# Two groups of eight head slots run as one matmul run, with the second group on the other column tiles and another PSUM bank

## The chip, the cores and the metric

The kernel runs on one core of one Trainium2 chip. The metric is the time of one execution on the device in microseconds (us), lower is better. Three runs of the kernel before gave 1065.8, 1064.63 and 1068.15 us; the median is 1065.8.

## The reference

Three stages follow one another: a delta-rule attention over 4 x 8 heads, 768 tokens and a head size of 48, and two feed-forward layers over all 3072 tokens (width 384, inner width 2048).

```python
# attention: B, H, S, D = 4, 8, 768, 48
k_n = k / (np.linalg.norm(k, axis=-1, keepdims=True) + 1e-06)
for t in range(S):
    y[:, :, t] = np.einsum('bhd,bhde->bhe', q[:, :, t], state)
    v_old = np.einsum('bhde,bhd->bhe', state, kt)
    state = state + bt[:, :, :, None] * np.einsum('bhd,bhe->bhde', kt, vt - v_old)
# first layer:  h = x @ w_in;  g = h / (1 + exp(-1.702 h));  x = g @ w_out
# second layer: h = max(x @ w_in, 0);  out = (h * h) @ w_out
```

## The kernel before

**Chunks and slots.** The 768 tokens are cut into 12 chunks of 64. The 32 heads sit as 16 slots of two heads: of one slot, one head has partitions 0 to 63 and the other 64 to 127. The 16 slots are two groups of eight (`g` 1 and 0), or four quarters of four. All the matmuls of the attention are fp32; each of them shows as two MATMUL instructions in the trace, so a run of 16 matmuls is "x32" there.

**One chunk of the attention** takes these steps on TensorE (PE); the letters are used in the rest of the text.

- **a** (`run_a`): keys and queries against keys, 64 x 64 tiles with 128 columns, one run of 8 matmuls for each of the four quarters; ScalarE (ACT) then copies 6 pieces out of PSUM for each. `load_kq` fetches a quarter (256 KB).
- the triangular solve: `solve_in` and `solve_norm` on VectorE (DVE), `solve_prep` (its last writes are those of `U`), `solve_loop` on GpSimd (POOL; 31 pairs of operations for chunks 4 to 11), then `finish`, whose last operation on DVE writes `Td`.
- **x** (`run_x`): the state's old prediction, 48 x 64 tiles; DVE subtracts it from `v_sb`.
- **W0**, **W1** (`run_w`, k = 0 and 1): the solved block `Td` against `v_sb`, 32 x 32 tiles; ACT copies four pieces of 32 partitions into `ws`.
- **G** (`run_g`), between the two: 32 x 32 tiles; four subtractions of 32 partitions on DVE.
- **y** (`run_y`): the output of the chunk, 128 rows x 48 columns, both column halves in turn.
- **s** (`run_s`): the new state, 64 x 48 tiles; four additions on DVE into `ws`.

In x, W0, G, W1 and s the loop `for g, ps, A, sl in groups()` makes one run of 16 matmuls for each group, into one of three PSUM banks (`a0` to `a2`, for chunks 2 and up) that `bank()` hands out in turn. Within such a run two tiles alternate: the head in the lower rows and the head in the upper rows, which write to different column halves.

```python
for g, ps, A, sl in groups():              # run_w
    for p in range(8):
        for h in range(2):
            r = 64 * h + 32 * k
            todo.append((ps[r:r + 32, p, :], Td[r:r + 32, 8 * g + p, :], v_sb[r:r + 32, 8 * g + p, :], True, True))
    mms((0.64, 0.82), todo, [("Td", n % 2), ("v", g, k)], [A], 0.25)
```

**The layers.** `step` issues the 9 matmuls of `h` (128 x 512; 128 x 256 at the start) for one slice of the inner width, and `layer2` the 9 of `z`. The results go through ACT (`g`, `ghi`) and DVE (`g`, `glo`) between the two. These large matmuls of the first layer are mixed with the attention of later chunks; `run_items` places the steps of a chunk at fixed steps of the layer (`TUNE["scan"]`, `TUNE["solve"]`, `gscan`, `gsolve`).

**The order.** Nothing is issued directly: every operation is put into `Program` with its cost, and `flush` writes the order of each engine out as a list scheduler that goes by these costs (for matmuls the first number given to `mms`, the second is the cost at the lower clock). Each engine then works through its list in order, so an instruction that waits holds up all that stand behind it on its engine.

Of the kernel before, what the change touches and what calls it, by code (L numbers as in the profile page):

```python
# [190 lines left out]
def kernel(  # L191
    ctx: ExitStack,
    tc: tile.TileContext,
    kq: bass.AP,
# [194 lines left out]
    def run_a(n, g, nxt=None):
        (t, keys), i = kq_of.pop((n, g)), n % 2  # L390
        G = G_sb[i]
        ps, A = bank(8 if n < 2 else 3)
        mms(0.87, [(ps[64 - r:128 - r, 128 * p:128 * p + 128], t[r:r + 64, 0, p, :], t[r:r + 64, :, p, :], True, True)
                  for p in range(4) for r in (64, 0)], keys + (["first"] if n == 1 else []), [A])
        if nxt:
            load_kq(*nxt)
        v4 = ps.rearrange("p (a c t) -> p a c t", a=4, c=2)
        sl = slice(4 * g, 4 * g + 4)
        for r in range(0, 128, 32):
            if r % 64 == 0:  # L400
                copy(256, [A], [("G", i, g, r)], G[r:r + 32, sl, :], v4[r:r + 32, :, 0, :])
            else:
                copy(128, [A], [("G", i, g, r)], G[r:r + 32, sl, 0:32], v4[r:r + 32, :, 0, 32:64])
        for h in range(2):
            r = 64 * h
            copy(256, [A], [("P", h, i, g)], pq[h][i][r:r + 64, sl, :], v4[r:r + 64, :, 1, :], early=-TUNE["p_late"] if n < 2 else 0)
        if g == 3 and n > 1:
            for h in range(2):
                mask_P(n, h)
# [198 lines left out]
    def groups():  # L608
        for g in (1, 0):
            ps, A = bank()  # L610
            yield g, ps[:, 0:8 * D].rearrange("p (a d) -> p a d", a=8), A, slice(8 * g, 8 * g + 8)

    def run_x(n):
        for g, ps, A, sl in groups():
            todo = []
            for p in range(8):
                a = 8 * g + p
                todo.append((ps[0:64, p, :], kT_sb[64:112, a // 4, a % 4, :], ws[0][64:112, a, :], True, True))
                todo.append((ps[64:128, p, :], kT_sb[0:48, a // 4, a % 4, :], ws[1][0:48, a, :], True, True))
            mms((1.24, 1.3), todo, KT + [("S", g)], [A], 0.2)  # L620
            tt(8 * D, [A], [("v", g, 0), ("v", g, 1)], v_sb[:, sl, :], v_sb[:, sl, :], ps, ALU.subtract)

    def run_w(n, k):
        Td = Td_sb[n % 2]
        for g, ps, A, sl in groups():
            todo = []
            for p in range(8):
                for h in range(2):
                    r = 64 * h + 32 * k
                    todo.append((ps[r:r + 32, p, :], Td[r:r + 32, 8 * g + p, :], v_sb[r:r + 32, 8 * g + p, :], True, True))  # L630
            mms((0.64, 0.82), todo, [("Td", n % 2), ("v", g, k)], [A], 0.25)
            for h in range(2):
                r = 64 * h + 32 * k
                copy(8 * D, [A], [("W", g, k, h)], ws[h][r:r + 32, sl, :], ps[r:r + 32], ("act", "dve") if n == 0 else "act")

    def run_g(n):
        G = G_sb[n % 2]
        for g, ps, A, sl in groups():
            todo = []
            for p in range(8):  # L640
                for h in range(2):
                    r = 64 * h
                    todo.append((ps[r + 32:r + 64, p, :], G[r:r + 32, 8 * g + p, 32:64], ws[h][r:r + 32, 8 * g + p, :], True, True))
            mms((0.43, 0.43), todo, G_keys(n) + [("W", g, 0, 0), ("W", g, 0, 1)], [A], 0.25)
            for h in range(2):
                r = 64 * h + 32
                tt(8 * D, [A], [("v", g, 1)], v_sb[r:r + 32, sl, :], v_sb[r:r + 32, sl, :], ps[r:r + 32], ALU.subtract)
# [33 lines left out]
    def run_s(n):  # L681
        for g, ps, A, sl in groups():
            todo = []
            for p in range(8):
# [4 lines left out]
            for h in range(2):
                q = 64 - 64 * h  # L690
                if n == 0:
                    act(8 * D, [A], [("S", g)], out=ws[h][q:q + 48, sl, :], in_=ps[q:q + 48])
# [90 lines left out]
    with tc.manual_schedule():  # L783
# [11 lines left out]
        for g in range(4):  # L795
# [13 lines left out]
        for g in range(4):  # L809
# [200 lines left out]
```

## Time and profile before

| | |
|---|---|
| median of three runs | 1065.8 us (1064.63 to 1068.15) |
| profiled execution, first to last instruction (span; the profile lists no other time of it) | 1063.8 us |
| PE busy | 1019.1 us, 96% |
| DVE / ACT / POOL busy | 587.3 (55%) / 529.5 (50%) / 326.6 us (31%) |
| mean granted TensorE clock, share of full | 0.977 |
| large matmuls `h` and `z` of 128 x 512, one | 0.38 to 0.42 us busy, a new one each 0.23 us |
| last attention matmul (chunk 11's y) | begins at 578.5 us |

Busy time of one matmul is longer than its share of the engine, since matmuls overlap: it is the distance between starts that counts. A line "x32" of the timeline is a run of 32 instructions from the first start to the modelled end of the last. In brackets stands the idle time before a line and what ended it.

### The profile page before, as it was taken

Reading aid. Unit: us, or ns where it says so; the run is one execution under the profiler, and the core shown is the slowest. Engines: PE = TensorE matmul, PEld = TensorE weight load, DVE = VectorE, ACT = ScalarE, POOL = GpSimd, SP = SyncE. Lnnn points to the kernel's source line nnn. Section 1 sums busy time; section 2 is a strip of 40 time slices with the busy share of each in tenths; the row PEclk is TensorE's granted clock in tenths of the full one; section 3 lists DMA queues with packets and bytes.
Section 4 is the critical chain, followed back from the end, with each engine's and each line's share of the span. In section 5 each row is a group of like instructions: output and inputs, shape, how many; then the busy total and the mean of one; then the engine's idle time right before and its main releaser. Section 6 shows DMA issues by size and latency. Waiting matters only on the chain.

```text
span 1063.8 us, 24037 instructions
## 1 busy us (share of the span) xinstructions
PE 1019.1 (96%) x9900; PEld 833.7 (78%) x9900; DVE 587.3 (55%) x1176; ACT 529.5 (50%) x1088; POOL 326.6 (31%) x667
## 2 busy tenths in 40 slices
PE   4888899999999999999999999999999999999998
PEld 3777787877878787888787778878888888888886
DVE  6788786574655646463744578775343343433332
ACT  4587566646475546546535556554333343333333
POOL 1265241687656581857280022211000000000000
PEclk7689899999999999999999999999999999999999
DMA  8365462313223122212100354431001010000000
GB/s 229 99 172 153 123 178 63 114 32 95 66 80 85 52 65 81 75 42 75 55 31 6 118 149 117 149 91 60 0 21 40 1 60 1 1 30 1 31 1 30
DMA packets 43982, 76.33 MB, mean 72 GB/s; under 512 B 6624, under 2 KB 19552, under 8 KB 43872
## 3 DMA queue, kind: packets, MB, share of 16 engines
q1 hardware_dynamic: 43776, 74.75, 23.9%
q8 instruction: 77, 1.26, 0.5%
q14 instruction: 33, 0.27, 0.1%
q10 hardware_dynamic: 96, 0.05, 0.0%
HBM read 64.16 MB, written 9.44 MB: 69 GB/s over the span
## 4 chain that ended last, share of the span: by engine, by line
PE 72%; DVE 10%; POOL 6%; ACT 6%; DMA 4%; issue 3%; SPq 1%; DVEq 0%; ACTq 0%; POOLq 0%
PE h L310 31%; PE z L310 30%; PE a L310 11%; POOL tmpp L554 3%; POOL U L557 3%; ACT G L275 1%; DMA kq<-in_kq 1%; DVE c L292 1%; DVE c L289 1%; DVE v_sb L285 1%; DVE g L292 1%; DVE kT_sb L295 1%; DVE gu L295 1%; DVE glo L285 1%; DMA xf_sb<-xs_sb 1%
## 5 line engine op out<-in xcount | busy, mean ns | idle before, releaser
L270 ACT ACTIVATE g<-h 128x512 f32<-128x512 f32 (+1 forms) x200 | 115.5, 579 | 245.5 <-PE h L310 241.7
L310 PE MATMUL z<-glo,wo_hi 128*128 128x512 f32 (+1 forms) x600 | 230.8, 385 | 2.1 <-DVE glo L285 2.0
L310 PE MATMUL z<-ghi,wo_hi 128*128 128x512 f32 (+1 forms) x600 | 231.5, 386 | 0.1
L310 PE MATMUL z<-ghi,wo_lo 128*128 128x512 f32 (+1 forms) x600 | 229.2, 382 | 0.0
L285 DVE TENSOR_TENSOR glo<-g,ghi 128x512 fp32r<-128x512 f32 (+1 forms) x200 | 137.2, 687 | 96.3 <-ACT ghi L270 94.9
L270 ACT ACTIVATE ghi<-g 128x512 fp32r<-128x512 f32 (+1 forms) x200 | 122.6, 614 | 125.1 <-DVE g L285 61.7
L285 DVE TENSOR_TENSOR g<-g,h 128x512 f32<-128x512 f32 x96 | 66.0, 688 | 157.6 <-ACT g L270 157.5
L310 PE MATMUL h<-x_hi,wi_hi 128*128 128x512 f32 (+1 forms) x312 | 129.5, 415 | 10.8 <-DVE g L292 6.4
L554 POOL TENSOR_TENSOR tmpp<-U,gu 128x126 f32<-128x126 f32 (+22 forms) x248 | 110.4, 445 | 95.4 <-DVE U L289 76.8
L310 PEld LDWEIGHTS z<-glo,wo_hi 128*128 128x128 f32 x600 | 113.4, 189 | 27.4 <-DVE glo L285 5.9
L310 PEld LDWEIGHTS z<-ghi,wo_hi 128*128 128x128 f32 x600 | 113.4, 189 | 23.7 <-ACT ghi L270 0.5
L310 PEld LDWEIGHTS z<-ghi,wo_lo 128*128 128x128 f32 x600 | 113.4, 189 | 21.5
L292 DVE SCALAR_TENSOR_TENSOR g<-g,h 128x512 f32<-128x512 f32 (+1 forms) x104 | 66.5, 641 | 109.1 <-ACT g L270 109.0
L310 PE MATMUL h<-x_lo,wi_hi 128*128 128x512 f32 (+1 forms) x312 | 119.0, 381 | 0.6 <-DVE x_lo L285 0.6
L310 PE MATMUL h<-x_hi,wi_lo 128*128 128x512 f32 (+1 forms) x312 | 118.8, 381 | 0.4 <-DVE wi_lo L285 0.4
L310 PE MATMUL h<-x_hi,vi_hi 128*128 128x512 f32 x288 | 112.4, 390 | 0.0
L310 PE MATMUL h<-x_hi,vi_lo 128*128 128x512 f32 x288 | 112.2, 389 | 0.0
L557 POOL TENSOR_TENSOR U<-U,tmpp 128x126 f32<-128x126 f32 (+22 forms) x248 | 104.4, 421 | 23.6 <-DVE U L289 4.5
L310 PEld LDWEIGHTS h<-x_hi,wi_hi 128*128 128x128 f32 x312 | 59.9, 192 | 32.4 <-DVE g L292 12.0
L310 PEld LDWEIGHTS h<-x_hi,wi_lo 128*128 128x128 f32 x312 | 60.2, 193 | 11.3 <-DVE wi_lo L285 0.6
L275 ACT ACTIVATE G<-a 32x256 f32<-32x256 f32 (+1 forms) x172 | 55.2, 321 | 26.5 <-PE a L310 24.5
L310 PEld LDWEIGHTS h<-x_lo,wi_hi 128*128 128x128 f32 x312 | 60.4, 194 | 8.6 <-DVE x_lo L285 1.1
(119 smaller groups left out, 1436.5 us busy)
## 6 DMA issues: line engine op xcount, KB each, us to landing
raw<-in_w_in SPq DMA_DIRECT2D x32, 384.0 KB, 3.3
raw<-in_w_out SPq DMA_DIRECT2D x32, 384.0 KB, 3.6
kq<-in_kq SPq DMA_DIRECT2D x44, 256.0 KB, 3.2
kT_sb<-in_kq SPq DMA_DIRECT2D x11, 512.0 KB, 3.7
k_sb<-in_kt SPq DMA_DIRECT2D x12, 384.0 KB, 4.5
v_sb<-in_vt SPq DMA_DIRECT2D x12, 384.0 KB, 3.2
xf_sb<-zd SPq DMA_DIRECT2D x18, 256.0 KB, 2.7
out<-zs SPq DMA_DIRECT2D x18, 256.0 KB, 2.0
```

The costliest lines, as they stand in the source:

```text
L270: pg.add("act", c_act(n), lambda e: e.activation(**kw), reads, writes, early)
L275: e.activation(out=out, in_=in_, func=AF.Copy)
L285: pg.add(queue, cost, lambda e: e.tensor_tensor(out=out, in0=in0, in1=in1, op=op), reads, writes, early)
L289: pg.add("dve", c_dve(n, True), lambda e: e.tensor_scalar(**kw), reads, writes, early)
L292: pg.add("dve", c_dve(n), lambda e: e.scalar_tensor_tensor(**kw), reads, writes, early)
L295: pg.add("dve", c_dve(n), lambda e: e.transpose(out=out, in_=in_), reads, writes)
L310: e.matmul(out=out, lhsT=lhsT, rhs=rhs, start=start, stop=stop)
L554: e.tensor_tensor(out=t, in0=U[:, lo:hi, j:j + 1].to_broadcast(shape), in1=gu[:, j + 1:, j:j + 1].rearrange("p i o -> p o i").to_broadcast ...
L557: e.tensor_tensor(out=U[:, lo:hi, j + 1:], in0=U[:, lo:hi, j + 1:], in1=t, op=ALU.add)
```

## The change

- `run_x`, `run_w`, `run_g` and `run_s` take both groups at once: `groups()` now returns a list with two banks, and one run of 32 matmuls goes through the slots with the groups and heads innermost. Group 1 writes to the column tiles it wrote to before, group 0 to the other ones (`o`), in the other bank. So four tiles alternate where two did.
- `run_a` takes two quarters at once (16 matmuls, two banks), the second with its tiles on the other columns. For the result to come out at the right partitions, the halves of the partitions of odd quarters are swapped beforehand on the host (`_crossed`), in a new input `kf` from which `load_kq` reads. The input `kq` stays for `load_kT` and `load_q`. Both loads for the second pair of quarters are issued after the first pair's matmuls.
- The evictions of group 0 read at `o`. In x the subtraction of group 0 becomes two of 64 partitions; the number of the others is unchanged.
- The costs told to the scheduler are new: x 1.2 (was 1.24 for each group), W 0.75 (0.64 each), G 0.75 (0.43 each), s 0.95 (0.98 each), a 1.0 for two quarters (0.87 each). A merged run reads the keys of both groups, so it stands behind the evictions of both.

```diff
 def run_a(n, g, nxt=()):
+        for p in range(4):
+            for e in range(2):
+                for r in (64, 0):
+                    o = r if e else 64 - r
+                    todo.append((ps_of[e][0][o:o + 64, 128 * p:128 * p + 128], tiles[e][r:r + 64, 0, p, :], tiles[e][r:r + 64, :, p, :], True, True))
+        mms((1.0, 1.75), todo, reads, [A for _, A in ps_of])
...
     def groups():
+        out = []
         for g in (1, 0):
             ps, A = bank()
-            yield g, ps[:, 0:8 * D].rearrange("p (a d) -> p a d", a=8), A, slice(8 * g, 8 * g + 8)
+            out.append((g, ps[:, 0:8 * D].rearrange("p (a d) -> p a d", a=8), A, slice(8 * g, 8 * g + 8)))
+        return out
...
     def run_x(n):
+        mms((1.2, 1.5), todo, KT + [("S", g) for g in range(2)], [A for _, _, A, _ in both], 0.4)
+        for g, ps, A, sl in both:
+            if g:
+                tt(8 * D, [A], [("v", g, 0), ("v", g, 1)], v_sb[:, sl, :], v_sb[:, sl, :], ps, ALU.subtract)
+                continue
+            for h in range(2):
+                r = slice(64 * h, 64 * h + 64)
+                tt(8 * D, [A], [("v", g, 0), ("v", g, 1)], v_sb[r, sl, :], v_sb[r, sl, :], ps[64 - 64 * h:128 - 64 * h], ALU.subtract)
...
     def run_w(n, k):
-        for g, ps, A, sl in groups():
-            todo = []
-            for p in range(8):
+        both, todo = groups(), []
+        for p in range(8):
+            for g, ps, A, sl in both:
                 for h in range(2):
                     r = 64 * h + 32 * k
-                    todo.append((ps[r:r + 32, p, :], Td[r:r + 32, 8 * g + p, :], v_sb[r:r + 32, 8 * g + p, :], True, True))
-            mms((0.64, 0.82), todo, [("Td", n % 2), ("v", g, k)], [A], 0.25)
+                    o = r if g else r ^ 32
+                    todo.append((ps[o:o + 32, p, :], Td[r:r + 32, 8 * g + p, :], v_sb[r:r + 32, 8 * g + p, :], True, True))
+        mms((0.75, 0.95), todo, [("Td", n % 2)] + [("v", g, k) for g in range(2)], [A for _, _, A, _ in both], 0.45)
...
     def run_g(n):
+                    o = r + 32 if g else r
+        mms((0.75, 0.95), todo, G_keys(n) + [("W", g, 0, h) for g in range(2) for h in range(2)], [A for _, _, A, _ in both], 0.45)
...
     def run_s(n):
+                    o = 64 - r if g else r
+        mms((0.95, 1.2), todo, ["k"] + ws_keys(0) + ws_keys(1), [A for _, _, A, _ in both], 0.6)
...
+def _crossed(a):
+    out = a.copy()
+    out[:, 1::2, :64], out[:, 1::2, 64:] = a[:, 1::2, 64:], a[:, 1::2, :64]
+    return out
```

**What it moves.** On PE, the start of W0 of chunk 9, before:

```order
L310 MATMUL z_71<-ghi_84,wo_hi 128x512
L310 MATMUL z_71<-glo_86,wo_hi 128x512
L310 MATMUL z_71<-ghi_84,wo_lo 128x512
L310 MATMUL a_74<-v_sb,Td_112 32x48 x16
L310 MATMUL a_72<-v_sb,Td_112 32x48 x16
L310 MATMUL h_67<-x_hi_80,wi_hi 128x512
```

and in the changed kernel (the two `a` rows come eight times in all):

```order
L311 MATMUL z_69<-ghi_85,wo_hi 128x512
L311 MATMUL z_69<-glo_87,wo_hi 128x512
L311 MATMUL z_69<-ghi_85,wo_lo 128x512
L311 MATMUL a_74<-v_sb,Td_112 32x48 x2
L311 MATMUL a_72<-v_sb,Td_112 32x48 x2
...
L311 MATMUL z_70<-ghi_85,wo_hi 128x512
```

The two banks no longer get one run after the other; they alternate by pairs of matmuls in a single run.

On DVE, the subtractions behind x of chunk 9 (`a_73` and `a_72` are the banks of x), before and now. Before:

```order
L285 TENSOR_TENSOR v_sb<-v_sb,a_73 128x384
L285 TENSOR_TENSOR sm_s<-gu_107,sm_y 128x32
L303 STREAM_TRANSPOSE kT_sb<-gu_108 128x8x32
L285 TENSOR_TENSOR sm_a<-sm_s 128x32
L303 STREAM_TRANSPOSE kT_sb<-gu_108 128x8x32
```

Now:

```order
L286 TENSOR_TENSOR v_sb<-v_sb,a_72 128x384
L304 STREAM_TRANSPOSE gu_107<-G_105 128x256
L286 TENSOR_TENSOR glo_86<-g_82,ghi_84 128x512
L290 TENSOR_SCALAR sm_y<-gu_107 128x32
L286 TENSOR_TENSOR v_sb<-v_sb,a_73 64x384
L290 TENSOR_SCALAR sm_y<-sm_y 128x32
L304 STREAM_TRANSPOSE kT_sb<-gu_108 128x8x32
L286 TENSOR_TENSOR sm_a<-sm_y 128x32
L286 TENSOR_TENSOR v_sb<-v_sb,a_73 64x384
```

Group 0's subtraction is cut in two, and the steps of the solve of the next chunk stand elsewhere between them.

The place of W0 also moves against the large matmuls. The writes of `U` of a chunk, which open its solve, stand behind one `glo` on DVE; the table counts what PE's list has from the first large matmul that reads this `glo` to W0 of the same chunk. All the attention runs a, x, W1, G, y, s of other chunks are in it, once or twice each.

| chunk | 4 | 5 | 6 | 7 | 8 | 9 | 10 | 11 |
|---|---|---|---|---|---|---|---|---|
| large matmuls, before | 134 | 101 | 146 | 125 | 155 | 128 | 155 | 125 |
| large matmuls, changed | 155 | 188 | 116 | 140 | 131 | 137 | 137 | 137 |

## Rows read from the trace of the kernel before

**Rows 1.** The table by stretches: length, busy us of each engine, PEclk, DMA share, GB/s.

```profile
350.00:400.00 50.00, 50.00 (x612) 40.53 (x610) 27.77 (x57) 25.44 (x55) 33.62 (x78) 1.00 0.21 57
410.20:413.60 3.40, 3.37 (x8) 2.17 (x9) 3.40 (x8) 0.64 (x1) 0.00 (x0) 0.50 0.00 0
600.00:1064.00 464.00, 458.21 (x2009) 376.16 (x2007) 214.03 (x347) 187.28 (x327) 24.91 (x23) 1.00 0.15 47
```

**Rows 2.** The waits of PE from 130 to 600 us: total, times, longest.

```profile
PE h L310 <- DVE g L292: 2.2, 4, 0.7
PE h L310 <- ACT x_hi L270: 2.0, 2, 1.0
PE a L310 <- DMA kq<-in_kq: 1.3, 1, 1.3
...
PE a L310 <- DVE Td L285: 0.6, 1, 0.6
```

**Rows 3.** The timeline of PE: a run G of one group, and W1 of both.

```profile
140.83 0.28 PE L310 MATMUL z<-ghi,wo_lo 128*128 128x256 f32 x1
141.04 0.87 PE L310 MATMUL a<-ws,G 32*32 32x48 f32 x32
141.84 0.50 PE L310 MATMUL h<-x_hi,wi_hi 128*128 128x512 f32 x1
142.17 0.39 PE L310 MATMUL h<-x_lo,wi_hi 128*128 128x512 f32 x1
...
145.12 1.55 PE L310 MATMUL a<-v_sb,Td 32*32 32x48 f32 x64
```

**Rows 4.** The timeline of PE: s, x and a, of one group or quarter and of two.

```profile
52.50 0.92 PE L310 MATMUL a<-ws,k_sb 64*48 64x48 f32 x32 [0.41 <-ACT xf_sb L270]
195.45 1.64 PE L310 MATMUL a<-ws,k_sb 64*48 64x48 f32 x64
261.78 2.07 PE L310 MATMUL a<-ws,kT_sb 48*64 48x48 f32 x64
346.41 1.09 PE L310 MATMUL a<-kq 64*64 64x128 f32 x16
350.42 1.96 PE L310 MATMUL a<-kq 64*64 64x128 f32 x32
357.34 1.14 PE L310 MATMUL a<-ws,kT_sb 48*64 48x48 f32 x32
```

**Rows 5.** The timeline of PE: a warming run, four-tile runs of chunk 2, three instructions of y.

```profile
23.71 4.81 PE L495 MATMUL a<-k_sb 128*96 128x384 f32 x8
...
125.37 1.26 PE L310 MATMUL a<-Td,G 32*32 32x16 f32 x128
...
148.04 0.22 PE L310 MATMUL a<-pqa,ws 128*48 128x64 f32 x1
148.05 0.22 PE L310 MATMUL a<-pqb,ws 128*48 128x64 f32 x1
148.10 0.22 PE L310 MATMUL a<-pqa,ws 128*48 128x64 f32 x1
```

**Rows 6.** The timeline, DVE and PE: `U`, `Td` and W0 of chunks 4 and 11.

```profile
192.95 0.37 DVE L289 TENSOR_SCALAR U<-sm_s,dup_sb 128x16 f32<-128x16 f32 x2
...
233.71 0.69 DVE L285 TENSOR_TENSOR Td<-kT_sb 128x512 f32<-128x512 f32 x1
...
234.45 1.55 PE L310 MATMUL a<-v_sb,Td 32*32 32x48 f32 x64
...
526.40 0.24 DVE L289 TENSOR_SCALAR U<-sm_s,dup_sb 128x16 f32<-128x16 f32 x1
...
563.00 0.69 DVE L285 TENSOR_TENSOR Td<-kT_sb 128x512 f32<-128x512 f32 x1
565.15 1.55 PE L310 MATMUL a<-v_sb,Td 32*32 32x48 f32 x64
```

**Rows 7.** Groups of instructions from 160 to 580 us: DVE and ACT evictions.

```profile
L285 DVE TENSOR_TENSOR v_sb<-v_sb,a 32x384 f32<-32x384 f32 x36 | 19.6, 553 | 12.1 <-PE a L310 9.0 <-ACT G L275 2.5
L285 DVE TENSOR_TENSOR v_sb<-v_sb,a 128x384 f32<-128x384 f32 x18 | 9.6, 532 | 1.0 <-PE a L310 1.0
L275 ACT ACTIVATE ws<-a 32x384 f32<-32x384 f32 x72 | 34.7, 481 | 31.2 <-PE a L310 29.7
```

**Rows 8.** The timeline of PE: a wait shortly before the clock fell.

```profile
408.29 0.50 PE L310 MATMUL h<-x_hi,wi_hi 128*128 128x512 f32 x1 [1.01 <-ACT x_hi L270]
```

More of the change, by code (lines that the diff above doesn't have):

```diff
@@ L193 @@
     tc: tile.TileContext,
+    kf: bass.AP,
     kq: bass.AP,
@@ L385, in load_kq, with run_a @@
             t, keys = kq_sb[g % 2], [("kq", g % 2)]
-        dma(t, kq[n, g], [], keys, 128 * 8 * C * 4)
+        dma(t, kf[n, g], [], keys, 128 * 8 * C * 4)
         kq_of[n, g] = t, keys
[L389 to L407, printed above, removed]
+    def run_a(n, g, nxt=()):
+        i, G = n % 2, G_sb[n % 2]
+        ps_of = [bank(8 if n < 2 else 3) for _ in range(2)]
+        todo, reads = [], ["first"] if n == 1 else []
+        tiles = []
+        for e in range(2):
+            t, keys = kq_of.pop((n, g + e))
+            tiles.append(t)
+            reads = reads + keys
+        for p in range(4):
+            for e in range(2):
+                for r in (64, 0):
+                    o = r if e else 64 - r
+                    todo.append((ps_of[e][0][o:o + 64, 128 * p:128 * p + 128], tiles[e][r:r + 64, 0, p, :], tiles[e][r:r + 64, :, p, :], True, True))
+        mms((1.0, 1.75), todo, reads, [A for _, A in ps_of])
+        for x in nxt:
+            load_kq(*x)
+        for e in range(2):
+            ps, A = ps_of[e]
+            v4 = ps.rearrange("p (a c t) -> p a c t", a=4, c=2)
+            sl = slice(4 * (g + e), 4 * (g + e) + 4)
+            for r in range(0, 128, 32):
+                if r % 64 == 0:
+                    copy(256, [A], [("G", i, g + e, r)], G[r:r + 32, sl, :], v4[r:r + 32, :, 0, :])
+                else:
+                    copy(128, [A], [("G", i, g + e, r)], G[r:r + 32, sl, 0:32], v4[r:r + 32, :, 0, 32:64])
+            for h in range(2):
+                r = 64 * h
+                copy(256, [A], [("P", h, i, g + e)], pq[h][i][r:r + 64, sl, :], v4[r:r + 64, :, 1, :], early=-TUNE["p_late"] if n < 2 else 0)
+        if g == 2 and n > 1:
@@ L617, in run_x @@
                 a = 8 * g + p
[L618 to L621, printed above, removed]
+                for h in range(2):
+                    q = 64 - 64 * h
+                    o = 64 * h if g else q
+                    todo.append((ps[o:o + 64, p, :], kT_sb[q:q + 48, a // 4, a % 4, :], ws[h][q:q + 48, a, :], True, True))
@@ L636, in run_g @@
     def run_g(n):
         G = G_sb[n % 2]
-        for g, ps, A, sl in groups():
-            todo = []
-            for p in range(8):
+        both, todo = groups(), []
+        for p in range(8):
+            for g, ps, A, sl in both:
                 for h in range(2):
                     r = 64 * h
-                    todo.append((ps[r + 32:r + 64, p, :], G[r:r + 32, 8 * g + p, 32:64], ws[h][r:r + 32, 8 * g + p, :], True, True))
-            mms((0.43, 0.43), todo, G_keys(n) + [("W", g, 0, 0), ("W", g, 0, 1)], [A], 0.25)
+                    o = r + 32 if g else r
+                    todo.append((ps[o:o + 32, p, :], G[r:r + 32, 8 * g + p, 32:64], ws[h][r:r + 32, 8 * g + p, :], True, True))
@@ L645, in run_g @@
+        mms((0.75, 0.95), todo, G_keys(n) + [("W", g, 0, h) for g in range(2) for h in range(2)], [A for _, _, A, _ in both], 0.45)
+        for g, ps, A, sl in both:
             for h in range(2):
                 r = 64 * h + 32
-                tt(8 * D, [A], [("v", g, 1)], v_sb[r:r + 32, sl, :], v_sb[r:r + 32, sl, :], ps[r:r + 32], ALU.subtract)
+                o = r if g else r - 32
+                tt(8 * D, [A], [("v", g, 1)], v_sb[r:r + 32, sl, :], v_sb[r:r + 32, sl, :], ps[o:o + 32], ALU.subtract)
@@ L794 @@
         load_v(0)
-        for g in range(4):
+        for g in (0, 2):
             run_a(0, g)
@@ L808 @@
             load_kq(1, g)
-        for g in range(4):
+        for g in (0, 2):
             run_a(1, g)
```

33 lines of the change are left out of this document (19 added, 14 removed).

## Prediction

> **What bounds the kernel now.** I read the table by stretches first. From 350 to 400 us PE is busy for all of 50 us at the full clock, with DVE at 28, ACT at 25 and POOL at 34 us; behind 600 us, with no attention left, PE is busy 458 of 464 us [rows 1]. So PE's list is the bound from about 130 us on, in both stretches. The waits of PE from 130 to 600 us are single ones, none over 1.3 us, and the attention's own are 1.3 us for a load and 0.6 us for `Td` [rows 2]. What PE no longer has to do there comes off the end, as long as its operands still arrive in time. The large matmuls do not change: 2009 in 464 us are 0.23 us each [rows 1]. What is left is the attention's share of PE, and the timeline gives its prices.
>
> **What one run costs.** A run G of one group takes 0.80 us from its first start to the next large matmul (141.04 to 141.84), and the large matmuls around it start 1.34 us apart (140.83 to 142.17) [rows 3]. Their own shares are 0.12 us for the half-width one and 0.23 us for the other, so the run costs 1.34 - 0.35 = 0.99 us. Two groups on end are busy 1.55 us against 0.87 us for one [rows 3]: the second adds 0.68 us, and getting into and out of a run costs 0.99 - 0.68 = 0.31 us. In the same way a second group adds 2.07 - 1.14 = 0.93 us to x, 1.64 - 0.92 = 0.72 us to s, and a second quarter 1.96 - 1.09 = 0.87 us to a [rows 4].
>
> **What the second group costs when it is merged.** Today two tiles alternate; the change makes it four, two on each half of the rows and two on each half (in W and G each quarter) of the columns. No row shows just that. The lower bound is nothing: the four tiles take as long as two. The upper bound is what the second group adds on end today, since every two neighbours of the new order are still the old pair. [...] In y both column halves use all 128 rows; `pqa` and `pqb` start at 148.04 and 148.05, and the next `pqa` at 148.10 [rows 5]. [...] And a run over four tiles that share nothing has 128 instructions in 1.26 us, 10 ns each, where G has 32 in 0.87 us, 27 ns each [rows 3, 5]: four tiles are kept busy by one list, and the issue is no limit at 10 ns. I take the lower bound. What stays open is two row halves that write the same columns, now in separate banks.
>
> [...]
>
> **The sum, part by part**, on PE from 130 us on (chunks 2 to 11):
>
> - W0 and W1: 20 merged pairs, 0.68 us each, 13.6 us; two of them stood apart today, which saves an entry of 0.31 us more each: 14.2 us.
> - G: 10 pairs at 0.68, three of them apart: 7.7 us.
> - x: chunks 3 to 11, 9 pairs at 0.93, seven apart: 10.5 us.
> - s: chunks 2 to 10, 9 pairs at 0.72: 6.5 us.
> - a: chunks 4 to 11, 16 pairs of quarters at 0.87, 13.9 us; the four quarters were three runs in seven chunks and are two now, 2.2 us: 16.1 us.
>
> That is 55.0 us. Before 130 us PE waits for DVE, ACT and loads much of the time, and of the some 14 us of matmul time that merging removes there (8 pairs of a, 2 of x, 6 of W and G, 2 of s) I take 4, with 0 and 14 as the ends. Sum: 59 us saved.
>
> **What comes back.**
>
> - *The solve.* W0 needs `Td`, at the end of a chain over POOL, ACT and DVE. From the writes of `U` it took 234.4 - 192.95 = 41.5 us in chunk 4, where W0 began 0.05 us after `Td` was done, and 563.7 - 526.4 = 37.3 us in chunk 11, with 1.5 us to spare [rows 6]. That chain does not get shorter. The work that covers it does: for chunk 6 the new order has 116 large matmuls between (27.2 us), and a twice, x, y, s, G and W1 at merged prices (8.7 us), 35.9 us. The same count gives 40.0 us for chunk 4, 42.5, 38.4, 41.8, 40.8 and 39.5 us for 7 to 11; chunk 5 starts behind chunk 4's solve and has 53.8. Against a middle chain of 39.4 us chunk 6 is short by 3.5 and chunk 8 by 1.0 us; against 41.5 us the five short ones lack 13 us in all, against 37.3 us 1.4. I take 5 us.
> - *The evictions.* With two runs, the first group's two evictions lay beside the second group's matmuls; a merged run has all four behind it, 4 x 0.553 us on DVE or 4 x 0.481 on ACT [rows 7], and G, W1, y and the next x stand behind them. The scheduler puts large matmuls between (eight to twelve, 1.9 to 2.8 us), about as long. Up to 0.5 us for four steps of ten chunks is 20 us, none is 0; I take 3, since such waits on the attention's copies are no row of the waits today [rows 2]. The additional subtraction in x costs DVE 0.55 us a chunk [rows 7], beside 22 of 50 us idle [rows 1].
> - *The clock.* [...] I count one such stretch more, 2 us, and up to three, 5 us.
> - *Loads.* Both loads of a second pair are issued behind the first pair's matmuls, with 12 to 21 large matmuls between the pairs, 2.8 to 4.9 us; a load cost 1.3 us of waiting once [rows 2]. It is in the rounding.
>
> 59 - 5 - 3 - 2 = 49 us. The profiled execution's span of 1063.8 us is 2.0 us below the median, which is the time outside the span and the scatter; the change touches neither, so I take 49 us off the median: **1017 us**. With the ends, 69 us saved and 2 lost give 999, 55 saved and 38 lost give 1049; not all ends come together, so this case's own range is 1003 to 1035.
>
> **The rivals.**
>
> - *A: the tiles take turns.* If tiles of one row half, or those that share columns, do not run together, only entries are saved: 0.31 us for the some 20 places where runs stood apart, 6 to 7 us: 1059 us. [...] 0.13.
> - *B: the waits take half.* The chain is 41.5 us in most chunks and the evictions cost their 0.5 us each: 13 + 15, with three clock stretches 33 us lost: 59 - 33 = 26, about 1040 us. For it is chunk 4's 0.05 us of slack [rows 6], against it that W0 of chunk 11 had 1.5 us. 0.10.
> - *C: slower, by the solve and the clock.* W0 of each of the eight chunks waits, and each wait is followed by a stretch at half clock of 1.7 us. It decides from 59 / 8 = 7.4 us a chunk, so from a wait of 5.7 us; at 6.5 us it gives 8 x 8.2 = 66 us lost and 1073 us. For it the chain must reach some 46 us, 4.5 above the longest row [rows 6]. With A it would need less than 1 us a chunk, which is the likelier way to it. 0.05.
> - The change does what it says: four tiles alternate in the order listed, so there is no rival in that.
>
> **How the numbers follow.** The forecast has 0.72, A 0.13, B 0.10, C 0.05. 0.3% is 3.2 us, about what a measurement of this kernel can tell from no change, so "same" is 1062.6 to 1069.0. A lies 4 us from that edge and sends 0.04 there. Faster: 0.72 + 0.10 + 0.09 = 0.91; same 0.04; slower 0.05. The range takes the forecast's own and B, and leaves A and C out: 1003 to 1049.
>
> **What would show it.** In the timeline, W and G "x64" near 0.90 us instead of 1.55, s near 0.95 (1.64), x near 1.15 (2.07), a "x32" near 1.1 (1.96). If they stay at the old lengths, A holds and the rest falls. The last attention matmul should begin near 530 us instead of 578.5, and the time from there to the end stay as it is. The waits of PE should list `Td` with about 5 us; over 12 us there, or over 10 us on `ws` and `v_sb` together, is B. The mean clock should stay at 0.97 or above. A time under 1000 us would say that the head gained as much as its matmul time.

## The result, and the profile after

The changed kernel takes 1048.8 us (median of four runs, 1046.38 to 1048.91) against 1065.4 us (1064.63 to 1068.15) for the kernel before in the same comparison: ratio 0.983, 95% interval 0.9805 to 0.9851. It is faster, by 17 us; the forecast was 49. The time lies at the upper end of the range, 32 us above the number. The times of the experiments below come from other sittings, in which the kernel before had medians of 1067.5 to 1068.8 us; differences of 2 or 3 us between sittings say nothing, and the ratios are the safer comparison. The profiled execution has a span of 1044.7 us and a mean granted clock of 0.961 (before 1063.8 and 0.977).

**The matmuls came out as priced.** The timeline of PE of the changed kernel (start, us, engine, line, operation, `x` instructions), one run of W, G, s, a and x, each with both groups or two quarters:

```profile
342.26 0.88 PE L311 MATMUL a<-v_sb,Td 32*32 32x48 f32 x64
346.03 0.88 PE L311 MATMUL a<-ws,G 32*32 32x48 f32 x64
355.04 0.94 PE L311 MATMUL a<-ws,k_sb 64*48 64x48 f32 x64
358.18 1.10 PE L311 MATMUL a<-kq 64*64 64x128 f32 x32
369.18 1.15 PE L311 MATMUL a<-ws,kT_sb 48*64 48x48 f32 x64
```

Before, the same work took 1.55, 1.64, 1.96 and 2.07 us (W, s, a, x) [rows 3, 4]. Four tiles run in the time of two (G 0.88 us against 0.87 for one group, s 0.94 against 0.92, a 1.10 against 1.09 for one quarter, x 1.15 against 1.14 [rows 3, 4]), also where they share columns, as in x, s and a (two row halves by two column halves). In W and G each of the four tiles has a column quarter of its own.

**The time went into idle PE and a lower clock.** Busy time by engine, from the page of the changed kernel:

```profile
PE 969.3 (93%) x9900; PEld 780.2 (75%) x9900; DVE 597.9 (57%) x1182; ACT 528.4 (51%) x1088; POOL 336.7 (32%) x672
```

PE is busy 49.8 us less than the 1019.1 us before. That this is near the 49 us of the forecast is chance: the 49 were what is left after the waits, and the matmul time to go was 55 us behind 130 us and some 14 ahead of it. And PE's idle time rose by 30.7 us: 1063.8 - 1019.1 = 44.7 before, 1044.7 - 969.3 = 75.4 now. 49.8 - 30.7 = 19.1 us is the difference of the spans. The table by stretches (columns as in [rows 1]) of the kernel before; its last stretch is in [rows 1]:

```profile
0.00:60.00 60.00, 39.06 (x749) 33.31 (x750) 44.91 (x145) 34.27 (x85) 17.84 (x31) 0.70 0.59 164
60.00:130.00 70.00, 60.09 (x1194) 53.86 (x1197) 58.38 (x139) 49.94 (x128) 29.96 (x60) 0.94 0.51 150
130.00:250.00 120.00, 116.98 (x1939) 93.68 (x1936) 82.87 (x169) 70.94 (x157) 67.86 (x143) 1.00 0.32 93
250.00:400.00 150.00, 147.98 (x1802) 118.91 (x1798) 82.10 (x172) 83.32 (x183) 97.67 (x219) 1.00 0.27 75
400.00:600.00 200.00, 196.80 (x2229) 157.80 (x2228) 105.03 (x206) 103.74 (x213) 88.37 (x194) 0.99 0.20 58
```

and of the changed kernel:

```profile
0.00:60.00 60.00, 28.40 (x732) 22.35 (x732) 44.86 (x143) 31.81 (x79) 18.03 (x30) 0.68 0.58 164
60.00:130.00 70.00, 56.30 (x1040) 49.18 (x1040) 54.75 (x117) 49.36 (x126) 31.43 (x63) 0.81 0.49 148
130.00:250.00 120.00, 111.16 (x1769) 88.11 (x1770) 83.89 (x182) 67.68 (x150) 59.47 (x124) 0.94 0.29 85
250.00:400.00 150.00, 137.61 (x2112) 106.28 (x2111) 92.10 (x186) 86.89 (x189) 96.60 (x208) 0.99 0.26 76
400.00:600.00 200.00, 195.59 (x2318) 152.45 (x2317) 122.67 (x238) 116.11 (x240) 108.78 (x230) 1.00 0.25 76
```

Length less busy time is the idle time: 20.9, 9.9, 3.0, 2.0 and 3.2 us before, 31.6, 13.7, 8.8, 12.4 and 4.4 us now. A third of the new idle time is in the first 60 us, another third from 250 to 400 us. The clock column fell from 0.94 to 0.81 between 60 and 130 us, and from 1.00 to 0.94 in the next stretch. Over the whole span, what is missing to the full clock grew from (1 - 0.977) x 1063.8 = 24.5 us to (1 - 0.961) x 1044.7 = 40.7 us, by 16.2 us. The part of it that falls on busy time is already in the 969.3 us.

**Which waits.** The waits of PE from 130 to 600 us, which before were 7.9 us in all [rows 2], are 26.9 us now, the largest of them:

```profile
PE h L311 <- DVE g L293: 8.0, 9, 1.8
PE a L311 <- DMA kq<-in_kf: 6.2, 8, 1.6
PE z L311 <- DVE glo L286: 4.8, 7, 2.0
PE a L311 <- DVE Td L286: 3.2, 2, 3.0
PE h L311 <- ACT x_hi L271: 2.0, 3, 1.1
PE a L311 <- ACT ws L276: 1.0, 3, 0.6
```

Of `Td`, 3.0 us is one wait of chunk 3, inside its solve (behind its x, ahead of its W0); W0 waits 0.2 us in all. More than half stands ahead of large matmuls (`h`, `z`), not of the attention's. One place shows how that can come about. PE from 270 us on (in brackets the idle time before and what ended it):

```profile
270.43 1.10 PE L311 MATMUL a<-kq 64*64 64x128 f32 x32
...
277.39 0.44 PE L311 MATMUL a<-kq 64*64 64x128 f32 x4 [1.53 <-DMA kq<-in_kf]
...
280.92 0.64 PE L311 MATMUL h<-x_hi,wi_hi 128*128 128x512 f32 x1 [1.81 <-DVE g L293]
281.35 0.63 PE L311 MATMUL h<-x_lo,wi_hi 128*128 128x512 f32 x1
```

and ACT at the same time:

```profile
273.94 1.34 ACT L271 ACTIVATE gu<-U,dup_sb 128x512 f32<-128x512 f32 x2 [4.88 <-POOL U L570]
275.30 1.32 ACT L276 ACTIVATE G<-a 32x256 f32<-32x256 f32 x4
276.63 0.38 ACT L276 ACTIVATE pqa<-a 64x256 f32<-64x256 f32 x1
277.02 0.38 ACT L276 ACTIVATE pqb<-a 64x256 f32<-64x256 f32 x1
277.42 1.32 ACT L276 ACTIVATE G<-a 32x256 f32<-32x256 f32 x4
278.75 0.38 ACT L276 ACTIVATE pqa<-a 64x256 f32<-64x256 f32 x1
279.14 0.38 ACT L276 ACTIVATE pqb<-a 64x256 f32<-64x256 f32 x1
279.54 1.08 ACT L271 ACTIVATE g<-h 128x512 f32<-128x512 f32 x2
```

The twelve copies of a merged pair of quarters are one block of 4.2 us on ACT, where a quarter had six; `g` stands behind all of them, and the next `h` waits for what DVE makes of `g`. But the copies came late too: their matmuls were done at 271.53 us, and ACT had stood idle for 4.88 us at the operation ahead of them in its list, `gu`, which waits for the last write of `U` by the solve on POOL. So `g` was held by the solve and by the copies, and this place does not tell them apart. PE's other wait there is for the next pair's load. From 281.10 to 284.50 us the granted clock is 0.50, and the large matmuls start 0.43 us apart.

Such waits of ACT for the solve are not rare. From 130 to 600 us they are, in the kernel before, the changed one, and three of the experiments below (`late_only`, `from3b`, `old_costs`):

```profile
ACT gu L270 <- POOL U L557: 8.1, 5, 3.4
ACT gu L271 <- POOL U L570: 14.3, 6, 4.9
ACT gu L271 <- POOL U L599: 6.9, 4, 2.5
ACT gu L271 <- POOL U L599: 17.1, 6, 4.4
ACT gu L271 <- POOL U L570: 32.3, 8, 6.0
```

All waits of PE in the same window are 7.9, 26.9, 18.0, 25.1 and 45.5 us. In these five short waits go with short ones and long with long, though not pair by pair (6.9 with 18.0, 8.1 with 7.9); which of them makes the other was not tried.

In the first 60 us the longest waits of PE on the attention's own operands are now:

```profile
PE a L311 <- ACT kT_sb L276: 7.5, 1, 7.5
PE a L311 <- DVE ws L278: 2.0, 2, 1.8
PE a L311 <- ACT xf_sb L271: 1.8, 1, 1.8
```

The wait for `kT_sb` was 2.6 us before. The last y begins at 559.97 us instead of 578.46 (the forecast had about 530); the time behind it did not change (484.7 us, before 485.3).

### The profile page after: what moved, and what is told of

It reads as the page before. It is cut to its first block, busy times and chain, and to the rows that moved or that the text cites. A ratio compares the mean times of both kernels' runs of the same rounds, so it can differ in the third digit from the quotient of the medians.

```text
span 1044.7 us, 24071 instructions
## 1 busy us (share of the span) xinstructions
PE 969.3 (93%) x9900; PEld 780.2 (75%) x9900; DVE 597.9 (57%) x1182; ACT 528.4 (51%) x1088; POOL 336.7 (32%) x672
## 4 chain that ended last, share of the span: by engine, by line
PE 57%; DVE 16%; POOL 10%; ACT 8%; issue 4%; DMA 3%; SPq 1%; DVEq 0%; ACTq 0%; POOLq 0%
PE z L311 26%; PE h L311 25%; PE a L311 5%; POOL tmpp L567 4%; POOL U L570 4%; ACT G L276 2%; DMA kq<-in_kf 2%; DVE v_sb L286 2%; DVE glo L286 2%; DVE g L293 2%; DVE c L290 1%; DVE c L293 1%; SPq L258 1%; ACT ws L276 1%; ACT ghi L271 1%
## 5 line engine op out<-in xcount | busy, mean ns | idle before, releaser
L286 DVE TENSOR_TENSOR glo<-g,ghi 128x512 fp32r<-128x512 f32 (+1 forms) x200 | 140.5, 704 | 100.3 <-ACT ghi L271 98.8
L311 PEld LDWEIGHTS z<-glo,wo_hi 128*128 128x128 f32 x600 | 113.8, 190 | 36.7 <-DVE glo L286 15.6
L567 POOL TENSOR_TENSOR tmpp<-U,gu 128x126 f32<-128x126 f32 (+22 forms) x248 | 113.5, 458 | 73.1 <-DVE U L290 54.7
L570 POOL TENSOR_TENSOR U<-U,tmpp 128x126 f32<-128x126 f32 (+22 forms) x248 | 108.3, 437 | 21.1 <-DVE U L290 2.1
L286 POOL TENSOR_TENSOR wo_lo<-c,wo_hi 128x384 fp32r<-128x384 f32 x21 | 22.6, 1075 | 132.4 <-ACT wo_hi L271 132.4
```

The costliest lines, as they stand in the source:

```text
L286: pg.add(queue, cost, lambda e: e.tensor_tensor(out=out, in0=in0, in1=in1, op=op), reads, writes, early)
L311: e.matmul(out=out, lhsT=lhsT, rhs=rhs, start=start, stop=stop)
L567: e.tensor_tensor(out=t, in0=U[:, lo:hi, j:j + 1].to_broadcast(shape), in1=gu[:, j + 1:, j:j + 1].rearrange("p i o -> p o i").to_broadcast ...
L570: e.tensor_tensor(out=U[:, lo:hi, j + 1:], in0=U[:, lo:hi, j + 1:], in1=t, op=ALU.add)
```

## The experiments

Eighteen kernels were run. In the table, idle is span less PE busy, and clock loss is (1 - granted clock) x span, each from that kernel's profiled execution; the ratio is to the kernel before, with its 95% interval.

| kernel | median us | ratio | PE busy | idle | clock loss |
|---|---|---|---|---|---|
| before | 1065.4 | | 1019.1 | 44.7 | 24.5 |
| the change | 1048.8 | 0.983 (0.9805 to 0.9851) | 969.3 | 75.4 | 40.7 |
| `a_only` | 1072.6 | 1.005 (1.0025 to 1.0071) | 1010.4 | 56.6 | 40.5 |
| `scan_only` | 1063.5 | 0.997 (0.9944 to 0.9987) | 990.4 | 73.7 | 39.4 |
| `head_apart` | 1055.9 | 0.989 (0.9857 to 0.9913) | 982.0 | 70.0 | 44.2 |
| `early_loads` | 1049.6 | 0.983 (0.9802 to 0.9852) | 974.5 | 72.6 | 53.4 |
| `after_costs` | 1061.0 | 0.992 (0.9893 to 0.9948) | 974.2 | 82.9 | 49.7 |
| `after_costs_early` | 1058.7 | 0.990 (0.9876 to 0.9925) | 973.7 | 82.4 | 54.9 |
| `before_costs` | 1081.8 | 1.011 (1.0079 to 1.0136) | 1029.5 | 51.4 | 40.0 |
| `run_twice` | 1099.8 | 1.028 (1.025 to 1.0308) | 1030.7 | 67.0 | 32.9 |
| `old_costs` | 1081.9 | 1.014 (1.0108 to 1.0164) | 984.7 | 97.7 | 55.2 |
| `twice_early` | 1060.4 | 0.994 (0.9913 to 0.9962) | 989.2 | 67.0 | 38.0 |
| `twice_late_b` | 1080.3 | 1.014 (1.0107 to 1.0163) | 1008.2 | 69.6 | 39.9 |
| `twice_late` | 1102.3 | 1.032 (1.0286 to 1.0361) | 1024.2 | 74.2 | 51.6 |
| `late_only` | **1036.7** | **0.972** (0.9685 to 0.9751) | 982.4 | 52.2 | 29.0 |
| `from3` | 1048.7 | 0.981 (0.9773 to 0.985) | 991.3 | 61.8 | 44.2 |
| `from3b` | 1048.3 | 0.983 (0.9802 to 0.9864) | 982.6 | 64.6 | 36.7 |
| `from6` | 1040.8 | 0.975 (0.9721 to 0.9782) | 993.2 | 46.1 | 28.1 |
| `from8` | 1053.8 | 0.987 (0.9839 to 0.9896) | 999.2 | 52.9 | 24.2 |
| `early_a` | 1044.8 | 0.980 (0.9775 to 0.9833) | 978.2 | 64.1 | 37.5 |

**Each half alone.** `run_a` merged, the rest as before; and the reverse.

```diff
 # a_only: x, W, G, s of each group apart
+    def run_x(n):
+        (run_x_apart if True else run_x_both)(n)
...
 # scan_only: each quarter of a apart, loads from kq
-        dma(t, kf[n, g], [], keys, 128 * 8 * C * 4)
+        dma(t, (kq if True else kf)[n, g], [], keys, 128 * 8 * C * 4)
...
```

> Only run_a is merged (chunks 0 to 11); x, W, G and s run group by group as before. The matmul time saved is a's 16.1 us plus the head's share. Theory L (what is given back is mostly the late loads of the second pair of quarters, 4.9 us more waiting, and the head): about 1056 us, with the load waits of 5 us or more still in the list. Theory E (given back behind the merged x, W, G, s, by evictions and the order): the full 16 us is kept, about 1049 us.

> Only x, W, G and s are merged; the quarters of a run one by one as before. 38.9 us of matmul time saved from 130 us on. Theory L: no late loads, so most of it stays: about 1032 us. Theory E: the waits of large matmuls on g and glo (12.8 us in the changed kernel) stay, about 1045 us.

Measured: 1072.6 and 1063.5; both theories missed both times. The a runs alone make the kernel 0.5% slower and the others alone 0.3% faster, though each half takes matmul time away; both bring idle time (11.9 and 29.0 us) and clock loss (some 15 us each). The two results do not add up to that of both together, 17 us.

**The head.** Chunks 0 and 1 as before the change:

```diff
-    def run_x(n):
+    def run_x_both(n):
...
+    def run_x(n):
+        (run_x_apart if n < 2 else run_x_both)(n)
 # the same in run_a (with kq), run_w, run_g, run_s
```

> As the changed kernel, but everything of chunks 0 and 1 runs group by group as before. Theory H (in the head PE is not the bound; the merged runs take activity from PE, the clock stays at half for 82 us in place of 48 and the head is 8 us later): first large matmul back at 55.7 us, half clock near 48 to 55 us, and the time falls by 8 to 12 us, to about 1038 us. Against it (the head is late because of the order or the evictions of later chunks): within 3 us of 1048.8.

Measured: 1055.9. The first large matmul starts at 55.1 us, as before the change (55.7; 60.6 with it), but 5 us gained at the start turn into 7 lost at the end: waits for `g` from 130 us on are 13.8 us instead of 8.0. So the late start of the layer is not by itself what the time is lost to.

**The loads.** The second pair of quarters gets two buffers of its own and is loaded with the first.

```diff
-            t, keys = kq_sb[g % 2], [("kq", g % 2)]
+            t, keys = (kq_sb, kq1_sb)[g // 2][g % 2], [(("kq", "kq1")[g // 2], g % 2)]
```

> As the changed kernel, but the second pair of quarters of a chunk has buffers of its own (those that chunk 1 uses) and is loaded with the first pair. Theory L: the waits on kq fall from 6.2 us behind 130 us to under 1.5 us and the time by 4 to 6 us, to about 1044 us. If the waits only move (PE then waits for DVE or ACT at the same place): within 2 us of 1048.8.

Measured: 1049.6, no gain. The waits for `kq` are gone, those for `g` have risen from 8.0 to 13.6 us and for `x_hi` from 2.0 to 4.1. The loads by themselves are not the cause.

**The numbers told to the scheduler.** Costs nearer to the measured durations, in the change and, as a control, in the kernel before.

```diff
-        mms((0.75, 0.95), todo, ...
+        mms((1.0, 1.3), todo, ...
 # a 1.2, x 1.25, s 1.05; ACT, DVE and POOL operations 0.05 to 0.1 us more each, transposes 0.14; large matmuls 8% more
```

> The changed kernel with other numbers told to the scheduler alone, nearer to the durations of the traces: ACT 0.165 and DVE 0.17 us plus their share for each element (were 0.08 and 0.07), POOL 0.27 (0.22), a transpose 0.70 (0.56), large matmuls 0.703 us for three (0.65), and for the merged runs a 1.2, x 1.25, W and G 1.0, s 1.05. Theory P (what is given back behind 130 us comes from the written order: it was laid out with costs of small DVE and ACT operations that are too low, and PE now arrives before them): the waits of PE on g, glo and x_hi behind 130 us fall from 14.8 to under 7 us and the time to about 1036 us. Theory M (merging itself makes the waits: four evictions behind every run, whatever the order): within 5 us of 1049, the waits about as long.

> The control: the kernel before with the same numbers told to the scheduler (its runs of one group as they measured: a 1.05, W and G 0.83, s 0.85; x 1.24 as it is). Its waits behind 130 us are 7.9 us, so by theory P little is to be had: 1060 to 1070 us. If it falls by as much as the changed kernel does, the costs are a gain of their own and say nothing on the change.

Measured: 1061.0 and 1081.8. No theory had either. Both orders are worse than the one they replace, by the ratios some 10 and 12 us, with not one matmul more: that much hangs on the order alone. Between the two the merge is worth 20.8 us, about as with the old numbers. With the early loads added, this version took 1058.7, ratio 0.990 (0.9876 to 0.9925), 2.3 us less and between the two expectations:

> Both edits: the scheduler's numbers as in after_costs and the second pair of quarters loaded with the first, in buffers of its own. Early loads alone left the time (1049.6), the waits having moved from the loads to g. Theory P: with an order that counts DVE and ACT rightly they are worth their 4 to 5 us, so 4 to 5 us under after_costs. Theory M: as after_costs within 2 us.

**The merged form at the old matmul time.** Each merged run is issued twice, and the scheduler is told the old costs of two runs.

```diff
-        mms((1.2, 1.5), todo, KT + ...
+        mms((2.48, 2.6), todo + todo, KT + ...
 # W 1.28, G 0.86, s 1.96, a 1.74; old_costs: the same costs, but todo once
```

> The changed kernel with every merged run issued twice over (the second writes the same results again) and the scheduler's costs set to those of two runs of before. So PE's time in these runs is again what it was before, and only the joint dependence on both groups and the order differ. Theory M (the joint evictions cost time by themselves): 10 us or more above before, 1078 us. Theory P or the clock (the waits and the half clock come because PE has less to do): about before, 1060 to 1072 us, with half clock near 48 us again and waits behind 130 us under 12 us.

> The merged runs as in the change, issued once, but the scheduler is told the sum of what the two runs cost before (x 2.48, W 1.28, G 0.86, s 1.96, a 1.74 us), so every engine's order is that of the kernel that issued its merged runs twice (1099.8 us) and only the matmul time differs. Theory M (the matmuls saved are worth their time wherever they stand): about 1049, the 51 us between that kernel and the change. Theory B (in the first 245 us other engines set the pace, so matmul time is worth nothing there): only what chunks 4 to 11 issue comes back, 30 to 37 us, 1063 to 1070. If the order that the smaller costs give is itself worth or costs something, the time differs from the change's 1048.8 by that amount.

Measured: 1099.8, at the PE busy time of the kernel before plus 12 us; what both groups in one run and the order that comes with it cost is here 22 us of idle time and 8 of clock. That is what theory M said. Taking the second issue away with the same order gave only 17.9 us (1081.9): 46 us of busy time went, 31 us of idle time and 22 us of clock loss came. The last 33 us to the change come from the order that its lower costs give. Theories M (1049) and B (1063 to 1070) both missed; what came is the third case of the expectation, an order that is itself worth something: matmul time is not worth itself in an order made for another.

**What PE's time is worth early and late.** The change in its own order, with the merged runs of some chunks issued twice.

```diff
-        mms((1.2, 1.5), todo, KT + ...
+        mms((1.2, 1.5), todo * (2 if n < 4 else 1), KT + ...
 # twice_late_b: n >= 4
```

> The change with its own costs and its own order on every engine, but the merged runs of chunks 0 to 3 are issued twice, which puts back some 17 to 20 us of matmul time at full clock (chunks 0 to 3 of 12, of the 51 us that issuing all twice cost), all of it before 270 us. Theory B (the first 245 us are paced by the conversions and copies on VectorE and ScalarE, TensorE has slack there): 1047 to 1055, and the half-clock stretches of the first 245 us shrink from 81.9 us. Theory M (TensorE paces those too): 1064 to 1071.

> The change with its own order; the merged runs of chunks 4 to 11 issued twice, and the transposes as in the change (in the earlier run of this kind those of chunks 4 to 11 had become one instruction and those of chunks 0 to 3 four, a second change). Theory B (TensorE is the bound from chunk 4 on): the 30 to 37 us of matmul time in full, 1079 to 1086. If TensorE has slack there too: 1060 to 1072. If the earlier run's 1102 was right: above 1090.

Measured: 1060.4 (+11.6 us) and 1080.3 (+31.5 us). DVE, ACT and POOL run the change's own lists in both. The busy lines of the two pages, `twice_early` and then `twice_late_b`:

```profile
PE 989.2 (94%) x11372; PEld 801.7 (76%) x11372; DVE 596.2 (56%) x1182; ACT 529.8 (50%) x1088; POOL 339.8 (32%) x672
```

```profile
PE 1008.2 (94%) x12908; PEld 822.4 (76%) x12908; DVE 595.2 (55%) x1182; ACT 530.1 (49%) x1088; POOL 336.8 (31%) x672
```

Early, 19.9 us of busy time more cost a span longer by 11.5 us (58%); late, 38.9 us cost 33.1 (85%). So PE's list is nearly the bound from chunk 4 on, and only half of one before: neither theory's number for the early chunks, but between them. The two sums also part the change's result. If they add up, which was not tried, the matmul time that merging saves is worth 43.1 us in this order; since the change gained 16.6, the new order and the joint runs cost some 26 us of it (an estimate from these two kernels).

**Merged from one chunk on.** As `head_apart`, with the border elsewhere.

```diff
-        (run_x_apart if n < 2 else run_x_both)(n)
+        (run_x_apart if n < 4 else run_x_both)(n)
 # late_only; from3b 3, from6 6, from8 8; early_a: 4, but run_a always merged
```

> Chunks 0 to 3 run apart as before the change, chunks 4 to 11 merged. Theory B (merging is worth nothing in the first 245 us, and the joint waits cost a little there): the 10 to 12 us by which the change runs behind the kernel before at 110 to 120 us do not appear, the gain of 18 us of the later chunks stays: 1040 to 1049. Theory M (the early merge is worth its matmul time too, only hidden by a poorer order): 1055 to 1062, since the matmul time of four chunks comes back. A rival on the order alone (any other order of the work loses some 12 us, as the two kernels with other costs did): 1055 to 1065 with the loss before 130 us, where this kernel's chunks are those of the kernel before.

> Chunks 0 to 7 apart as before, chunks 8 to 11 merged. Theory B (late merging is worth its matmul time, 29 us over chunks 4 to 11 in the run before, 3.6 a chunk): 1051 (four chunks, 14.6 us). Theory of the order alone (any new order falls where it falls, within some 10 us either way): anywhere from 1045 to 1065 with no regular step from one cut to the next.

> Chunks 0 to 5 apart as before, chunks 6 to 11 merged. Theory B: 1043.5 (six chunks at 3.6 us). Theory of the order alone: 1035 to 1060, off the line between 1051 and 1037.

> Chunks 0 to 2 apart, 3 to 11 merged, as the run of that cut before, but the transposes of chunk 3 stay one instruction as in both kernels (the earlier run cut them in four from chunk 3 on as well, so it changed two things). Theory B with its border at chunk 4: 1040 to 1050. If the transposes made its loss: 1033 to 1036.

> The a runs merged in all chunks, x, W, G and s merged from chunk 4 on only. Against 1036.7 with both apart in chunks 0 to 3 and 1048.8 with both merged. If the early loss is in the a runs (a pair needs both its quarters, and takes both load buffers): 1045 to 1052. If it is in the joint scan runs (x, W, G and s need the state, the solve and the evictions of both groups at once): 1034 to 1040. If each half loses when the other stays apart, as the two halves did over all chunks: above 1052.

`late_only` takes 1036.7 us, ratio 0.972 (0.9685 to 0.9751), and beats both kernels; its interval lies wholly under the change's (0.9805 to 0.9851); theory B had 1040 to 1049. Its table by stretches:

```profile
0.00:60.00 60.00, 37.71 (x750) 32.64 (x750) 45.03 (x145) 34.31 (x85) 18.02 (x31) 0.74 0.60 165
60.00:130.00 70.00, 62.92 (x1060) 56.60 (x1063) 53.54 (x124) 47.29 (x120) 27.04 (x58) 0.83 0.49 147
130.00:250.00 120.00, 115.71 (x1895) 91.85 (x1883) 85.96 (x185) 70.04 (x155) 69.13 (x137) 0.99 0.31 90
250.00:400.00 150.00, 139.92 (x2093) 107.20 (x2093) 92.02 (x186) 94.62 (x211) 102.73 (x217) 1.00 0.28 84
400.00:600.00 200.00, 196.05 (x2241) 154.72 (x2241) 124.30 (x243) 110.59 (x222) 96.62 (x207) 1.00 0.25 76
```

Idle are 22.3, 7.1, 4.3, 10.1 and 3.9 us. Against the change, PE does 13.1 us more and idles 23.2 us less, 15.9 of them before 130 us. Against the kernel before, 36.7 us of busy time less give 29.2 us of span. Its waits from 130 to 600 us are those on the layers and the loads again, and shorter:

```profile
PE h L311 <- DVE g L293: 7.4, 9, 1.2
PE z L311 <- DVE glo L286: 4.4, 5, 2.7
PE a L311 <- DMA kq<-in_kf: 3.0, 3, 1.4
```

From the border at 8 over 6 to 4 the time falls from 1053.8 over 1040.8 to 1036.7; theory B had 1051 and 1043.5 for the first two. Those two have a second edit, whose share was not measured: the border from which a chunk's transposes are cut in four moved with it. The same holds for two more runs, a border at 3 (1048.7) and the late runs issued twice (1102.3):

> Chunks 0 to 2 apart as before, chunks 3 to 11 merged. Chunks 0 and 1 alone apart gave 1055.9, 0 to 3 apart 1036.7. Theory B with its border at about 245 us (chunk 3 lies ahead of it): 1038 to 1050, since a merged chunk there costs what it saves or more. If chunk 3 is worth as much as the later ones: 1033. Theory of the order alone: 1040 to 1060.

> The change with its own order; the merged runs of chunks 4 to 11 are issued twice, those of chunks 0 to 3 once (the mirror of the kernel that issued the early ones twice, which lost 11.6 us). Issuing all twice at the old costs lost 51. Theory B (TensorE is the bound from chunk 4 on): 30 to 37 us more than the change, 1079 to 1086. If the later chunks too have slack on TensorE: 1060 to 1072.

`from3b` and `twice_late_b` repeat these without it. The transposes made nothing of the loss at 3 (1048.3), but 22 us of the 1102.3. With them fixed, merging chunk 3 as well costs 11.6 us: idle time rises by 12.4 us, spread over 60 to 400 us, and PE's busy time does not fall, since what it saves is lost to the clock (36.7 instead of 29.0 us). `early_a` takes 1044.8: the a runs of chunks 0 to 3 cost some 8 of the 12 us between `late_only` and the change. (Its interval, 0.9775 to 0.9833, overlaps the change's, so the other 4 are not clear of noise.) The row of borders 0, 2, 3, 4 (1048.8, 1055.9, 1048.3, 1036.7) isn't even, so there is scatter from the order in it. Each of these kernels has another order on every engine. In the change's own order the matmul time saved in chunks 0 to 3 is worth 11.6 us (`twice_early`); that leaving them apart gains 12 us all the same is thus some 24 us of order and joint dependence, and no run here parts the two.

## Why the prediction was right and where it was wrong

- **The bound and the prices: right.** A second group merged costs nothing: W and G 0.88 us, s 0.94, x 1.15, a 1.10, each within 0.05 us of what was given for it. Rival A, by which W of both groups would have stayed at 1.55 us, falls, and C with it: the kernel is faster. That the second group would cost nothing was an estimate, from the starts of y and from a run whose four tiles share nothing [rows 5]; no row of before showed four tiles that share rows. One working on the way is loose and touches nothing: 116 large matmuls at 0.23 us are 26.7 us, not 27.2.
- **The sum saved: right, what it is worth not.** 49.8 us less busy time, and up to 16.2 us more lost to the clock within it, make up to 66 us of matmul time gone, against 55 from 130 us on and 14 ahead of it. The forecast took 59 of these as time; by the kernels issued twice they are worth some 43.
- **The solve: the 5 us did not come where they were looked for.** W0 waited 0.2 us for `Td`, and chunk 3's solve 3.0 us. But the chain was not covered with room to spare: `Td` was done 0.05 to 0.9 us before W0 in all of chunks 4 to 11. In chunk 6 it took 42.1 us from the writes of `U`, and the cover, counted as 35.9 us, came to 42.6 because 6.3 us of PE's other waits lie in it (the two ends, beside the W0 at 342.26 us above):

```profile
299.64 0.37 DVE L290 TENSOR_SCALAR U<-sm_s,dup_sb 128x16 f32<-128x16 f32 x2
340.95 0.80 DVE L286 TENSOR_TENSOR Td<-kT_sb 128x512 f32<-128x512 f32 x1
```

  By this count, taking those waits away would have moved them to W0. The chain also holds ACT's list, as at 273.94 us.
- **The evictions: the named waits small, the step wrong.** Waits on `ws`, `v_sb` and `xf_sb` from 130 us on are 2.4 us, as forecast (3). But what stands behind them in the lists, or behind a wait for the solve, is late: waits for `g`, `glo`, `ghi` and `x_hi` came to 15.1 us there (before 5.3). The forecast asked who waits for the evictions, not who is queued behind them on ACT and DVE.
- **"It is in the rounding": wrong.** Loads cost 6.2 us of waits from 130 us on against 1.3 [rows 2]. Yet with the waits gone (`early_loads`) the time stayed, so this was no sum to be paid for singly.
- **The clock: 2 us forecast, 16.2 measured.** The mean is 0.961, where 0.97 or above was forecast. The step looked at stretches from 130 us on; most of the loss is ahead of 250 us, where the granted clock of 60 to 130 us fell from 0.94 to 0.81. No run shows the 2 us as a cost of this change: they stand for one more stretch like that of 410.20 to 413.60 us, 3.40 us at 0.50 [rows 1] and so 1.7 us lost. From 130.90 to 600 us the kernel before has that stretch alone; the changed one has three, 17.0 us and so 8.5 us lost:

```profile
130.90:137.70 6.80, 6.80 (x152) 6.54 (x151) 5.39 (x21) 2.75 (x8) 1.53 (x2) 0.50 0.24 61
171.90:178.70 6.80, 5.86 (x164) 4.71 (x165) 5.50 (x10) 2.25 (x6) 1.69 (x2) 0.50 0.01 4
281.10:284.50 3.40, 3.40 (x9) 2.63 (x9) 1.05 (x2) 3.29 (x10) 0.00 (x0) 0.50 0.18 70
```

- **The head: 4 us of gain forecast, none came.** The first large matmul starts 4.9 us later than before, and by 130 us the changed kernel has run 1772 matmul instructions instead of 1943. 0 was taken as the worst end; it was a loss.
- **The step that failed** is the list "What comes back" as a whole: 5 + 3 + 2 = 10 us, each for a wait with a name. It came to 30.7 us of idle time and 16.2 us of clock. The new order of every engine, which the section on the change had shown, had no term in the list; by the kernels issued twice it and the joint runs cost some 26 us. Rival B's number (1040) is nearer, but its mechanism is not what happened: by its own test, over 12 us on `Td` or over 10 on `ws` and `v_sb` (3.2 and 1.7 were measured), it falls. That the time lies within the range is luck: the end at 1049 stands for 13 us on `Td`, 20 on the evictions and 5 of clock, and the loss did not come in these parts.

Shown is where the change is behind `late_only`: two thirds of the idle time that `late_only` does not have lies before 130 us, and with chunks 0 to 3 merged as well PE is busy 13.1 us less and idle 23.2 us more. The cause stays open: neither the wait through which it comes is settled, nor whether it is the joint runs or only the order that the scheduler made for them. Removing one wait (the loads, the head) moved it to another, and the order alone was good for 10 to 33 us. Not tried were an order of ACT in which `gu` does not stand ahead of a pair's copies, other steps of the layer at which the merged runs are placed, and a split of the twelve copies of a pair.

## What to carry to other kernels

Matmul time taken from a list is worth its length only where the list is the bound: here 81 to 85% late and 58% early. Issuing the doubtful instructions twice in one stretch, in an unchanged order, prices that for this order. Here it paid to merge only there and to keep the old form elsewhere. When two short runs become one, ask what stands behind their doubled block of copies on the copying engine, and what stands ahead of it and waits, and count the idle time and the clock of each stretch in the sum, not only the waits that have a name.

## What the runs showed of the hardware that was not expected

Two row halves that write the same columns, in separate PSUM banks, took no longer than one in these runs: the point left open in the forecast. The 64 instructions of a merged x take 1.15 us and those of s 0.94 us, where 32 took 1.14 and 0.92 before; 32 of a take 1.10 us, where 16 took 1.09 [rows 4].

The granted clock does not follow PE's idle time alone. The change idles more ahead of 250 us than the kernel before and was granted less there, and from 86.60 to 100.30 us it ran at 0.50, after 6.60 us in which PE was busy for 6.01. But from 60 to 130 us `late_only` idles 7.1 us and was granted 0.83, while the kernel before idles 9.9 us at 0.94 and `from3b` 12.4 us at 0.90:

```profile
60.00:130.00 70.00, 57.59 (x1168) 51.38 (x1168) 58.21 (x132) 48.78 (x125) 28.39 (x60) 0.90 0.50 149
80.00:86.60 6.60, 6.01 (x204) 5.21 (x205) 3.28 (x6) 5.36 (x17) 0.90 (x1) 1.00 0.51 158
86.60:100.30 13.70, 12.09 (x223) 10.29 (x223) 12.64 (x38) 7.76 (x18) 3.46 (x4) 0.50 0.48 147
```
